# Pairing the heads of two batches by the engine of their scores, and opening layer two's memory nine steps earlier

## The chip, the cores and the metric

The kernel runs on one core of a Trainium2 chip. The metric is the device time of one execution in microseconds; the time before is 929.59 us, the median of three runs (927.67 to 930.28). TensorE is called PE in the rows, VectorE DVE, ScalarE ACT, GpSimd POOL, SyncE SP.

## The reference, cut to what matters

An attention of 4 batches, 8 heads, 576 positions and 64 values per head is followed by two feed-forward layers on 2304 tokens (512 to 2048 to 512). The attention is the sum of two: one over q, k and v pooled by four positions (144 by 144), and one over a band of seven keys around each position.

```python
def sm_attn(qq, kk, vv):
    s = scale * np.matmul(qq, kk.transpose(0, 1, 3, 2))
    s = s - np.max(s, axis=-1, keepdims=True)
    a = np.exp(s)
    a = a / (np.sum(a, axis=-1, keepdims=True) + 1e-09)
    return np.matmul(a, vv)
q_d = q.reshape(B, H, Sd, factor, D).mean(axis=3)
out_up = np.repeat(sm_attn(q_d, k_d, v_d), factor, axis=2)
mask = np.abs(pos[:, None] - pos[None, :]) < factor
scores = np.where(mask, scale * np.matmul(q, k.transpose(0, 1, 3, 2)), -1000000000.0)
...
attn_out = (out_up + out_local).astype(np.float32)
x = attn_out.transpose(0, 2, 1, 3).reshape(B * S, H * D)
h = x @ w_in;  x = (np.maximum(h, 0.0) + alpha * np.minimum(h, 0.0)) @ w_out
h = x @ w_in2; g = np.where(h > 0.0, h, np.exp(np.minimum(h, 0.0)) - 1.0)
out = g @ w_out2
```

`k_d` and `v_d` are made as `q_d`; `out_local` is softmax(scores) times v.

## The kernel before, in words

**Stages.** Layer 1 is the backbone: 2304 tokens in eight groups of 288, two per batch, and for each group 16 tiles of the 2048 hidden values. One tile is a *step*; there are 128, numbered from 0, and from step 32 on each group is 16 steps (groups of batch three at 64 and 80, of batch four at 96 and 112). A step has twelve input matmuls (`mm_in`, L415; 128x288, operands split into a high and a low part, `xh`, `xl`, `wi`), an activation on ACT and DVE (`th_elem`, L1422: `n`, `r`, `gh`, `gl`) and, two steps later, twelve output matmuls (`out1`, L1450; `gh`, `gl`, `wo`). Layer 2 works in 40 *units* u of four per turn of 512 tokens (`upf` L1706, `down2` L1743): seven products of half size in place of eight, on `xq` and `wi`, then the output with `wo`.

**Attention** of a batch runs between the matmuls of the group before. Its heads are taken in four pairs p of two. Per pair the q and k (`qk`) and v (`vv`) are loaded, pooled by DVE, and the pooled attention is computed (`th_pair` L1066, `th_da` L1103): scores `sm`, softmax `P`, its transposes `pt`, v transposed `vs`, and the weighted sum (`dav_mm` L761, two heads on the two halves of the output's rows), copied to `od` by ACT (`dav_ev` L770). The banded scores of a pair are eight blocks of 72 queries by 78 keys (`s_mm` L569): a matmul with 64 rows of contraction per block and head, four blocks to a bank, copied by ACT to `ss` (`s_ev` L578), written to DRAM `scr` (`s_write` L585) and read back as a band `sd`. In batches three and four (b = 2 and 3 in the code) only head 1 of each pair goes that way; head 0 is scored by DVE (`SDVE` L91, `th_SD` L1041, `s_dve` L533), from its own loads `kls` and `qls`. In batch two both heads go to PE. Band softmax and weighted sum of batches three and four are DVE's (`acc`, `pr`, `vl`); PE transposes `acc` (`x_tp` L797) and DVE adds `od` into `x`, which the next group reads. While layer 1 runs, attention has two PSUM banks.

**Order.** No engine's order is written by hand. `fused_kernel` keeps threads with a priority each, and a clock of its own (`_Clock`, L94) with a cost for every operation: PE work of a thread is put between layer 1's matmuls when the clock has its operands ready (`pe`, L918), ACT and DVE work when those engines come to it (`advance`, L876). For a matmul of a head in the upper half of the array's rows the clock counts 8 ns (L265), since it takes its partner to run beside it; for a load it counts a byte per 1/360 ns (L232). All loads go through SP's one queue, in program order.

**Memory.** Attention's tiles are in a pool `pA`. At step T7 = 112 (L821, L1880) it is closed, layer 2's pool `pC` takes its place, and layer 2's threads start: `th_ldw2` (L1364) loads raw weights into slots that layer 1 sets free one by one from step 112 on, `decode` (L1309) makes them 32 bits wide (`cp` on ACT, `cp` and `cw` on DVE), `th_conv_in` (L1331) forms four differences `S` and four split tiles `wi`, `th_conv_out` (L1355) two `wo` per set of weights, and `th_x2` (L1502) prepares the tokens `x`, `xt`, `xq`.

Of the kernel before, what the change touches and what calls it, by code (L numbers as in the profile page):

```python
# [7 lines left out]
F32 = mybir.dt.float32  # L8
# [3 lines left out]
U64 = mybir.dt.uint64  # L12
# [6 lines left out]
S = 576  # L19
D = 64  # L20
# [23 lines left out]
DP = -14.7  # L44
NP0 = -14.6
STEP = 1.0
G2 = 512
U2 = G2 // 2
XR = 11
# [39 lines left out]
PN = 1, 5  # L89
NB = 2  # L90
SDVE = {2: (0,), 3: (0,)}  # L91


class _Clock:  # L94
# [208 lines left out]
def fused_kernel(ctx: ExitStack, tc: tile.TileContext, qk, vt, vl, ql, kl, vb, w_in1, w_out1, alpha,  # L303
# [281 lines left out]
    def s_write(b, p, k0, n, t, rs):  # L585
        for i, r in enumerate(rs):
            u0 = p * (NU // 2) + k0
            SP.dma_start(out=scr[b, r][u0:u0 + n, 0:BLK * KW].rearrange("u (q k) -> q u k", k=KW), in_=t[:, i, 0:n])

    def band(t):  # L590
# [179 lines left out]
    def dav_ev(key, bk):  # L770
        b, p, qs = key
        if ("od", b) not in st:
            st["od", b] = Ap.tile([128, NP, SD], F32, tag="od", name="od", bufs=2)
        ACT.activation(out=st["od", b][:, p, qs[0] * 72:(qs[-1] + 1) * 72], in_=bk[:, 0:len(qs) * 72], func=AF.Copy)

    def av_ops(b, u, i):
        t0 = u * HT + i * TS
# [81 lines left out]
    def finish(*key):  # L859
        done[key] = ck.cur["t"]  # L860
# [157 lines left out]
                SP.dma_start(out=xsp, in_=st["x", 0, 0].rearrange("p k t j -> p k (t j)"))  # L1018

    def th_S(b, p):  # L1020
        rs = tuple(r for r in range(2) if r not in SDVE.get(b, ()))
        yield "key", "ld", b, p
        for i in range(2):
            yield "tok", "ss"
            bks = yield "bank", len(rs)
            s_mm(b, p, 4 * i, 4, bks, rs)
            if i == 1:
                finish("smm", b, p)
            yield ("ACT",)
            t = s_ev(4, bks)  # L1030
            release(bks)
            yield ("SP",)
            if b < NB:
                s_write0(b, p, i, t)
                finish("S", b, p, i)
            else:
                s_write(b, p, 4 * i, 4, t, rs)
            put("ss")
        finish("S", b, p)
# [19 lines left out]

    def th_qk(b, p):  # L1060
        yield "key", "sq", b, p
        if len(SDVE.get(b, ())) < 2:
            yield "key", "smm", b, p
        put("qk")

# [37 lines left out]
    def th_da(b, p, qs):  # L1103
        key = (b, p, qs)
        yield "tok", "P"
        bks = yield "bank", 2
        sd_mm(b, p, qs, bks)
        if b:
            put("sm")
        yield ("ACT",)  # L1110
        sd_ev(key, bks)
        release(bks)
        yield ("DVE",)
        sd_max(key)
        yield ("ACT",)
        sd_exp(key)
        yield ("DVE",)
        sd_rec(key)
        yield ("DVE",) if b < DN else ("ACT",)
        sd_norm(key, b < DN)  # L1120
        yield "tok", "pt"
        bks = yield "bank", 2
        pt_mm(key, bks)
        put("P")
        yield ("ACT",)
        pt_ev(key, bks)
        release(bks)
        yield "key", "vs", b, p
        bks = yield "bank", 1
        dav_mm(key, bks[0])  # L1130
        put("pt")
        if b:
            put("vs")
        else:
            finish("dav", p, qs)
        yield ("ACT",)
        dav_ev(key, bks[0])
        release(bks)
        finish("od1", b, p, qs)
        if all(("od1", b, z, qs) in done for z in range(NP)):  # L1140
            finish("od", b, qs[-1])

    def th_da0(p):
        yield "key", "sq", 0, p
# [22 lines left out]
    def th_soft(b):  # L1167
        yield "key", "sal", b
        for r in range(2):
            if r in SDVE[b]:  # L1170
                for u in range(2):
                    for i in range(HT // TS):
                        yield "key", "SD", b, u, i, r
            else:
                for p in range(NP):
                    yield "key", "S", b, p
        yield ("SP",)
        s_read(b)
# [183 lines left out]
        finish("wo", q, z)  # L1362

    def th_ldw2():  # L1364
        for q in range(NQ):
            for nm, z in (("i", 0), ("i", 1), ("o", 0), ("o", 1)):
                slot = wslot[q % NJ][z + (4 if nm == "o" else 0)]
                yield "key", "fr", q // NJ, slot
                yield ("DMA",)
                key = (2, nm, q % NP2 * 2 + z, q)  # L1370
                load_w(key, slot)
                finish("ld", key)
                ck.cur["t"] = now[0]

# [432 lines left out]
    with tc.manual_schedule():  # L1807
# [37 lines left out]
            spawn(th_conv(k), k / CS, early=ECONV)  # L1845
        for b in range(1, B):
            g0 = 32 * (b - 1)
            for p in range(NP):
                if len(SDVE.get(b, ())) < 2:
                    spawn(th_S(b, p), g0 + OS + p if b > 1 else P1 + p / 4)  # L1850
                spawn(th_qk(b, p), -20)
                spawn(th_pair(b, p), g0 + OP + p if b > 1 else P1 + p / 4, g0 + 2 * p + OPS if b > 1 else ST1 + ST2 * p)
            if b < NB:
                for u in range(2):
                    q = PN[u] + 32 * (b - 1)
# [18 lines left out]
        for s in range(NS1):  # L1874
            slot[0] = s if s else -1
            ly, g, f, first, last, i = seq[s]
            if s == 1:
                avail[:] = bank[6:8]
                banks[:] = [x for x in banks if any(x[0] is z for z in avail)]
            if s == T7:  # L1880
                assert all(t["p"] < -50 for t in threads), [t["w"] for t in threads]
                pA.__exit__(None, None, None)
                pC = tc.tile_pool(name="pC", bufs=1)
# [86 lines left out]
def _prepare(np, a):  # L1970
# [4 lines left out]
    for i, x in enumerate((q, k)):  # L1975
        qk[:, :, :, i, HALO:HALO + S] = x.transpose(0, 1, 3, 2).reshape(B, NP, 128, S)
    vt = v.transpose(0, 1, 3, 2).reshape(B, NP, 128, S)
    vp = np.zeros((B, H, SPAD, D), f4)
    vp[:, :, HALO:HALO + S] = v
    vl = np.stack([vp[:, :, NT * j:NT * j + NT + 2 * HALO] for j in range(CH)], axis=2)  # L1980
# [67 lines left out]
```

## Time and profile before

| what | value |
|---|---|
| median of three runs (lowest, highest) | 929.59 us (927.67, 930.28) |
| the profiled execution, its span | 928.21 us, 926.4 us |
| TensorE matmuls in flight; weight loads | 903.6 us (98%); 831.4 us (90%) |
| DVE, ACT, POOL busy | 721.1 us (78%), 523.3 us (56%), 2.9 us |
| moved by DMA | 106.36 MB, 115 GB/s mean |
| granted clock of TensorE, mean | 0.99 |

The span runs from the first to the last instruction; 1.8 us of the execution lie around it. Matmuls are pipelined, so a busy TensorE is not one at its peak, and the cost of a matmul in a stream is the distance between starts. An idle engine that nobody waits for costs nothing; a wait of TensorE does, in this kernel.

### The profile page before, as it was taken

Reading aid. Unit: us, or ns where it says so; the run is one execution under the profiler, and the core shown is the slowest. Engines: PE = TensorE matmul, PEld = TensorE weight load, DVE = VectorE, ACT = ScalarE, POOL = GpSimd, SP = SyncE. Lnnn points to the kernel's source line nnn. Section 1 sums busy time; section 2 is a strip of 40 time slices with the busy share of each in tenths; the row PEclk is TensorE's granted clock in tenths of the full one; section 3 lists DMA queues with packets and bytes.
Section 4 is the critical chain, followed back from the end, with each engine's and each line's share of the span. In section 5 each row is a group of like instructions: output and inputs, shape, how many; then the busy total and the mean of one; then the engine's idle time right before and its main releaser. Section 6 shows DMA issues by size and latency. Waiting matters only on the chain.

```text
span 926.4 us, 17510 instructions
## 1 busy us (share of the span) xinstructions
PE 903.6 (98%) x6721; PEld 831.4 (90%) x6721; DVE 721.1 (78%) x1552; ACT 523.3 (56%) x1312; POOL 2.9 (0%) x6
## 2 busy tenths in 40 slices
PE   8798999999999999999999998999999999999998
PEld 5577989999998999999999997899998988899987
DVE  6788986438778899899537999979797559989753
ACT  6798786645335642323236667656675456756543
POOL 0000000000000000000100000000000000000000
PEclk8899999999999999999999999999999999999999
DMA  9757816443122413010113751414324144242502
GB/s 267 274 213 270 273 31 97 125 132 100 46 71 66 145 49 107 27 37 32 47 36 106 227 186 54 155 46 137 98 85 125 36 157 140 84 160 80 182 12 79
DMA packets 69417, 106.36 MB, mean 115 GB/s; under 512 B 26610, under 2 KB 43378, under 8 KB 69154
## 3 DMA queue, kind: packets, MB, share of 16 engines
q1 hardware_dynamic: 69334, 105.25, 36.8%
q8 instruction: 52, 0.85, 0.4%
q14 instruction: 31, 0.25, 0.1%
HBM read 86.89 MB, written 19.78 MB: 115 GB/s over the span
## 4 chain that ended last, share of the span: by engine, by line
PE 80%; DVE 6%; ACT 6%; DMA 5%; issue 2%; SPq 0%; DVEq 0%; ACTq 0%
PE bank L298 80%; DMA qk<-in_qk_dram 2%; DMA rawi<-in_w_in_dram 1%; ACT dP L298 1%; DVE cw L298 1%; ACT wo L298 1%; DVE cp L298 1%; DVE wi L298 1%; DMA out_dram<-os 1%; ACT cp L298 1%; ACT n L298 1%; ACT cw L298 1%; ACT wi L298 1%; DVE gl L298 1%; ACT P L298 1%
## 5 line engine op out<-in xcount | busy, mean ns | idle before, releaser
L298 PE MATMUL bank<-xh,wi 128*128 128x288 f32 x976 | 223.8, 300 | 0.6 <-DVE wi L298 0.6
L298 PE MATMUL bank<-gh,wo 128*128 128x288 f32 x976 | 222.2, 299 | 1.3 <-ACT ys L298 1.3
L298 PEld LDWEIGHTS bank<-xq,wi 128*128 128x128 f32 x1536 | 195.7, 192 | 10.8 <-ACT wi L298 2.0
L298 PE MATMUL bank<-xq,wi 128*128 128x256 f32 x1536 | 198.7, 284 | 3.5 <-ACT wi L298 1.6
L298 ACT ACTIVATE n<-bank 128x288 f32<-128x288 f32 (+1 forms) x176 | 70.6, 401 | 200.0 <-PE bank L298 197.8
L298 PE MATMUL bank<-wo,gh 128*128 128x512 f32 x576 | 179.3, 392 | 0.1
L298 PEld LDWEIGHTS bank<-gh,wo 128*128 128x128 f32 x976 | 165.0, 188 | 5.0 <-ACT ys L298 2.1
L298 PEld LDWEIGHTS bank<-xh,wi 128*128 128x128 f32 x976 | 164.8, 188 | 4.8 <-issue 2.7
L298 PE MATMUL bank<-gl,wo 128*128 128x288 f32 x488 | 144.6, 296 | 0.3 <-DVE gl L298 0.2
L298 PE MATMUL bank<-xl,wi 128*128 128x288 f32 x488 | 143.7, 294 | 0.0
L298 PEld LDWEIGHTS bank<-wo,gh 128*128 128x128 f32 x576 | 103.3, 189 | 17.8 <-ACT gh L298 0.3
L298 PE MATMUL bank<-wo,gl 128*128 128x512 f32 x288 | 112.3, 390 | 0.2 <-DVE gl L298 0.2
L298 DVE SCALAR_TENSOR_TENSOR r<-n,nal,bank 128x288 f32<-128x288 f32 x128 | 65.2, 510 | 57.9 <-ACT n L298 57.2
L298 PEld LDWEIGHTS bank<-gl,wo 128*128 128x128 f32 x488 | 92.0, 188 | 0.8 <-DVE gl L298 0.8
L298 PEld LDWEIGHTS bank<-xl,wi 128*128 128x128 f32 x488 | 92.0, 188 | 0.2
L298 ACT ACTIVATE gh<-r 128x288 fp32r<-128x288 f32 x122 | 54.1, 443 | 65.3 <-DVE r L298 65.2
L298 DVE TENSOR_TENSOR gl<-r,gh 128x288 fp32r<-128x288 f32 x122 | 55.4, 454 | 17.4 <-ACT gh L298 16.9
L298 PEld LDWEIGHTS bank<-wo,gl 128*128 128x128 f32 x288 | 54.1, 188 | 12.5 <-DVE gl L298 0.8
L298 DVE TENSOR_TENSOR gl<-n,gh 128x512 fp32r<-128x512 f32 (+1 forms) x80 | 50.6, 634 | 9.4 <-ACT gh L298 8.5
L298 DVE TENSOR_TENSOR c<-m,bank 128x256 f32<-128x256 f32 x64 | 26.4, 419 | 36.0 <-PE bank L298 35.7
L298 ACT ACTIVATE gh<-n 128x512 fp32r<-128x512 f32 (+1 forms) x80 | 46.3, 582 | 12.4 <-DVE n L298 12.0
L298 ACT ACTIVATE n<-n 128x512 f32<-128x512 f32 (+1 forms) x80 | 47.2, 590 | 2.5
(125 smaller groups left out, 1215.0 us busy)
## 6 DMA issues: line engine op xcount, KB each, us to landing
rawi<-in_w_in_dram SPq DMA_DIRECT2D x40, 512.0 KB
rawo<-in_w_out_dram SPq DMA_DIRECT2D x40, 512.0 KB
qk<-in_qk_dram SPq DMA_DIRECT2D x12, 582.0 KB
x<-yT SPq DMA_DIRECT2D x8, 576.0 KB
osp<-os SPq DMA_DIRECT2D x18, 256.0 KB
os<-osp SPq DMA_DIRECT2D x18, 256.0 KB
out_dram<-os SPq DMA_DIRECT2D x18, 256.0 KB
yT<-ys SPq DMA_DIRECT2D x28, 144.0 KB
```

Source lines behind the costliest of these rows:

```text
L298: return fn(*args, **kw)
```

## The change

**Heads.** For batches three and four the host puts the eight heads in the order 0, 2, 4, 6, 1, 3, 5, 7. Pairs 0 and 1 then hold the four heads that DVE scores, pairs 2 and 3 the four that PE scores, and a score block has both heads of a pair (`th_S` only for pairs 2 and 3; `th_qk` lets the load of pairs 0 and 1 go behind the pooling). Pairs are taken in the order 0, 2, 1, 3. Since pairs 0 and 2 share two output tiles of heads in their first order, the weighted sum of the pooled attention waits for both (`th_dav`) and is one block of eight matmuls with one copy.

**Memory.** `pA` is closed at step TC = 103 in place of 112; an assertion there says that no thread of attention is left. Layer 2's first six raw tiles go to the buffers `n`, `gh`, `gl` of `pC` (`raws`), which layer 2 needs later, and wait for no weight slot.

```diff
--- before.py
+++ after.py
@@ -44,6 +44,8 @@
 DP = -14.7
 NP0 = -14.6
 STEP = 1.0
+TC = 103
+STG = ("n", "gh", "gl", "n", "gh", "gl")
 G2 = 512
 U2 = G2 // 2
 XR = 11
@@ -89,6 +91,8 @@
 PN = 1, 5
 NB = 2
 SDVE = {2: (0,), 3: (0,)}
+QUAD = {2, 3}
+QORD = 0, 2, 1, 3
 
 
 class _Clock:
@@ -585,6 +589,8 @@
     def s_write(b, p, k0, n, t, rs):
         for i, r in enumerate(rs):
             u0 = p * (NU // 2) + k0
+            if b in QUAD:
+                u0, r = (2 * p + r - NP) * (NU // 2) + k0, 1
             SP.dma_start(out=scr[b, r][u0:u0 + n, 0:BLK * KW].rearrange("u (q k) -> q u k", k=KW), in_=t[:, i, 0:n])
 
     def band(t):
@@ -772,6 +778,21 @@
         if ("od", b) not in st:
             st["od", b] = Ap.tile([128, NP, SD], F32, tag="od", name="od", bufs=2)
         ACT.activation(out=st["od", b][:, p, qs[0] * 72:(qs[-1] + 1) * 72], in_=bk[:, 0:len(qs) * 72], func=AF.Copy)
+
+    def dav2_mm(b, i, bk):
+        t = {(r, e): st.pop(("pt", r, b, i + e * (NP // 2), (0, 1))) for r in range(2) for e in range(2)}
+        for r in range(2):
+            for kh in range(2):
+                for e in range(2):
+                    PE.matmul(out=bk[e * D:(e + 1) * D, r * SD:(r + 1) * SD],
+                              lhsT=st["vs", b, i + e * (NP // 2)][:, kh, r * D:(r + 1) * D], rhs=t[r, e][:, kh, :],
+                              start=(kh == 0), stop=(kh == 1))
+
+    def dav2_ev(b, i, bk):
+        if ("od", b) not in st:
+            st["od", b] = Ap.tile([128, NP, SD], F32, tag="od", name="od", bufs=2)
+        ACT.activation(out=st["od", b][:, 2 * i:2 * i + 2], in_=bk[:, 0:2 * SD].rearrange("q (a k) -> q a k", a=2),
+                       func=AF.Copy)
 
     def av_ops(b, u, i):
         t0 = u * HT + i * TS
@@ -1018,7 +1039,7 @@
                 SP.dma_start(out=xsp, in_=st["x", 0, 0].rearrange("p k t j -> p k (t j)"))
 
     def th_S(b, p):
-        rs = tuple(r for r in range(2) if r not in SDVE.get(b, ()))
+        rs = (0, 1)
         yield "key", "ld", b, p
         for i in range(2):
             yield "tok", "ss"
@@ -1059,7 +1080,7 @@
 
     def th_qk(b, p):
         yield "key", "sq", b, p
-        if len(SDVE.get(b, ())) < 2:
+        if b not in QUAD or p >= NP // 2:
             yield "key", "smm", b, p
         put("qk")
 
@@ -1125,6 +1146,9 @@
         yield ("ACT",)
         pt_ev(key, bks)
         release(bks)
+        if b in QUAD:
+            finish("pt", b, p)
+            return
         yield "key", "vs", b, p
         bks = yield "bank", 1
         dav_mm(key, bks[0])
@@ -1140,6 +1164,23 @@
         if all(("od1", b, z, qs) in done for z in range(NP)):
             finish("od", b, qs[-1])
 
+    def th_dav(b, i):
+        for p in (i, i + NP // 2):
+            yield "key", "pt", b, p
+            yield "key", "vs", b, p
+        bks = yield "bank", 1
+        dav2_mm(b, i, bks[0])
+        for z in range(2):
+            put("pt")
+            put("vs")
+        yield ("ACT",)
+        dav2_ev(b, i, bks[0])
+        release(bks)
+        for p in (i, i + NP // 2):
+            finish("od1", b, p, (0, 1))
+        if all(("od1", b, z, (0, 1)) in done for z in range(NP)):
+            finish("od", b, 1)
+
     def th_da0(p):
         yield "key", "sq", 0, p
         yield from th_da(0, p, (0, 1))
@@ -1172,7 +1213,7 @@
                     for i in range(HT // TS):
                         yield "key", "SD", b, u, i, r
             else:
-                for p in range(NP):
+                for p in range(NP // 2 if b in QUAD else 0, NP):
                     yield "key", "S", b, p
         yield ("SP",)
         s_read(b)
@@ -1362,13 +1403,20 @@
         finish("wo", q, z)
 
     def th_ldw2():
+        k = 0
         for q in range(NQ):
             for nm, z in (("i", 0), ("i", 1), ("o", 0), ("o", 1)):
                 slot = wslot[q % NJ][z + (4 if nm == "o" else 0)]
-                yield "key", "fr", q // NJ, slot
+                key = (2, nm, q % NP2 * 2 + z, q)
+                if k >= len(STG):
+                    yield "key", "fr", q // NJ, slot
                 yield ("DMA",)
-                key = (2, nm, q % NP2 * 2 + z, q)
-                load_w(key, slot)
+                if k < len(STG):
+                    raw[key] = cp["pool"].tile([128, 512], U64, tag=STG[k], name="raws", bufs=2)
+                    SP.dma_start(out=raw[key], in_=wsrc[2, nm][key[2]])
+                else:
+                    load_w(key, slot)
+                k += 1
                 finish("ld", key)
                 ck.cur["t"] = now[0]
 
@@ -1845,11 +1893,15 @@
             spawn(th_conv(k), k / CS, early=ECONV)
         for b in range(1, B):
             g0 = 32 * (b - 1)
-            for p in range(NP):
-                if len(SDVE.get(b, ())) < 2:
-                    spawn(th_S(b, p), g0 + OS + p if b > 1 else P1 + p / 4)
+            for z in range(NP):
+                p = QORD[z] if b in QUAD else z
+                if b not in QUAD or p >= NP // 2:
+                    spawn(th_S(b, p), g0 + OS + z if b > 1 else P1 + z / 4)
                 spawn(th_qk(b, p), -20)
-                spawn(th_pair(b, p), g0 + OP + p if b > 1 else P1 + p / 4, g0 + 2 * p + OPS if b > 1 else ST1 + ST2 * p)
+                spawn(th_pair(b, p), g0 + OP + z if b > 1 else P1 + z / 4, g0 + 2 * z + OPS if b > 1 else ST1 + ST2 * z)
+            if b in QUAD:
+                for i in range(NP // 2):
+                    spawn(th_dav(b, i), g0 + OP + 2 * i + 1)
             if b < NB:
                 for u in range(2):
                     q = PN[u] + 32 * (b - 1)
@@ -1877,7 +1929,7 @@
             if s == 1:
                 avail[:] = bank[6:8]
                 banks[:] = [x for x in banks if any(x[0] is z for z in avail)]
-            if s == T7:
+            if s == TC:
                 assert all(t["p"] < -50 for t in threads), [t["w"] for t in threads]
                 pA.__exit__(None, None, None)
                 pC = tc.tile_pool(name="pC", bufs=1)
@@ -1975,6 +2027,11 @@
     for i, x in enumerate((q, k)):
         qk[:, :, :, i, HALO:HALO + S] = x.transpose(0, 1, 3, 2).reshape(B, NP, 128, S)
     vt = v.transpose(0, 1, 3, 2).reshape(B, NP, 128, S)
+    for b in QUAD:
+        hs = [0, 2, 4, 6, 1, 3, 5, 7]
+        vt[b] = v[b, hs].transpose(0, 2, 1).reshape(NP, 128, S)
+        for i, x in enumerate((q, k)):
+            qk[b, :, :, i, HALO:HALO + S] = x[b, hs].transpose(0, 2, 1).reshape(NP, 128, S)
     vp = np.zeros((B, H, SPAD, D), f4)
     vp[:, :, HALO:HALO + S] = v
     vl = np.stack([vp[:, :, NT * j:NT * j + NT + 2 * HALO] for j in range(CH)], axis=2)
```

PE, the first scores of batch three (`bank<-qk`), in steps 33 and 34. Before, two blocks of one head:

```order
L298 MATMUL bank_71<-xh,wi_651 128x288
L298 MATMUL bank_73<-qk 72x78 x4
L298 MATMUL bank_71<-xh,wi_651 128x288
L298 MATMUL bank_71<-xl,wi_651 128x288
L298 MATMUL bank_71<-xh,wi_651 128x288
L298 MATMUL bank_72<-qk 72x78 x4
L298 MATMUL bank_71<-xh,wi_651 128x288
L298 MATMUL bank_71<-xl,wi_651 128x288
L298 MATMUL bank_71<-xh,wi_651 128x288
```

Now:

```order
L302 MATMUL bank_70<-xh,wi_734 128x288
L302 MATMUL bank_72<-qk 72x78
L302 MATMUL bank_73<-qk 72x78
L302 MATMUL bank_72<-qk 72x78
L302 MATMUL bank_73<-qk 72x78
L302 MATMUL bank_72<-qk 72x78
L302 MATMUL bank_73<-qk 72x78
L302 MATMUL bank_72<-qk 72x78
L302 MATMUL bank_73<-qk 72x78
L302 MATMUL bank_70<-xh,wi_734 128x288
```

The rows alternate between two banks, one per head; the other three blocks of a batch read alike.

ACT, steps 102 to 104 of layer 1 (`n` opens a step). Before:

```order
L298 ACTIVATE n<-bank_70 128x288
L298 ACTIVATE gh<-r 128x288
L298 ACTIVATE n<-bank_71 128x288
L298 ACTIVATE gh<-r 128x288
L298 ACTIVATE n<-bank_70 128x288
L298 ACTIVATE gh<-r 128x288
```

Now:

```order
L302 ACTIVATE n<-bank_70 128x288
L302 ACTIVATE gh<-r 128x288
L302 ACTIVATE cp<-raws 128x512 x2
L302 ACTIVATE n<-bank_71 128x288
L302 ACTIVATE cp<-raws 128x512 x2
L302 ACTIVATE gh<-r 128x288
L302 ACTIVATE cp<-raws 128x512
L302 ACTIVATE n<-bank_70 128x288
L302 ACTIVATE cp<-raws 128x512
L302 ACTIVATE gh<-r 128x288
```

Six copies `cp` of staged tiles stand between the `gh` of layer 1; on SP their loads `raws` follow the result writes of batch three and stand ahead of the loads of `x`.

DVE, layer 2, between the `m` of u=2 and the `m` of u=3 (`wi` is the low part of a weight tile that u=3 reads). Before, the last 12 of 32 rows:

```order
L298 TENSOR_TENSOR wi_7228<-cw,wi_7228 128x512
L298 SCALAR_TENSOR_TENSOR n<-n,c 128x512
L298 TENSOR_TENSOR gl<-n,gh 128x512 x2
L298 TENSOR_TENSOR wi_7246<-S,wi_7246 128x512
L298 TENSOR_SCALAR cp<-cp 128x512
L298 SCALAR_TENSOR_TENSOR cw<-rawi_7021,cp 128x512
L298 TENSOR_SCALAR cp<-cp 128x512
L298 TENSOR_TENSOR wi_7256<-S,wi_7256 128x512
L298 SCALAR_TENSOR_TENSOR cw<-rawo_7069,cp 128x512
L298 TENSOR_TENSOR wi_7263<-cw,wi_7263 128x512
L298 TENSOR_SCALAR cp<-cp 128x512
L298 SCALAR_TENSOR_TENSOR cw<-rawi_7044,cp 128x512
```

Now, the first 12 of 23:

```order
L302 TENSOR_TENSOR m<-s_7138,bank_70 128x256
L302 TENSOR_TENSOR xq_7114<-xt,xq_7114 128x512
L302 TENSOR_TENSOR e<-m,bank_71 128x256
L302 TENSOR_TENSOR c<-e,bank_72 128x256
L302 TENSOR_TENSOR wi_7146<-cw,wi_7146 128x512
L302 TENSOR_TENSOR xt<-x_6845 128x512
L302 TENSOR_TENSOR gl<-n,gh 128x512
L302 TENSOR_SCALAR cp<-cp 128x512
L302 TENSOR_TENSOR wi_7183<-S,wi_7183 128x512
L302 SCALAR_TENSOR_TENSOR cw<-rawo_6988,cp 128x512
L302 TENSOR_TENSOR xq_7186<-xt,xq_7186 128x512
L302 TENSOR_TENSOR c<-m,bank_71 128x256
```

The first two `wi` move from the 21st and 24th row to the 5th and 9th; the `cp`, `cw` and `S` of later tiles leave this stretch.

## Rows read from the trace of the kernel before

**Rows 1.** The page: busy time by engine; the chain that ended last, by engine.

```profile
PE 903.6 (98%) x6721; PEld 831.4 (90%) x6721; DVE 721.1 (78%) x1552; ACT 523.3 (56%) x1312; POOL 2.9 (0%) x6
...
PE 80%; DVE 6%; ACT 6%; DMA 5%; issue 2%; SPq 0%; DVEq 0%; ACTq 0%
```

**Rows 2.** Waits of PE, 180 to 480 us: total us, times, longest.

```profile
PE bank L298 <- DMA qk<-in_qk_dram: 0.3, 1, 0.3
PE bank L298 <- ACT P L298: 0.2, 1, 0.2
```

**Rows 3.** Timeline of PE: start us, us, instruction, xcount; batch three's scores.

```profile
253.46 0.29 PE L298 MATMUL bank<-gh,wo 128*128 128x288 f32 x1
253.68 0.77 PE L298 MATMUL bank<-qk 64*72 64x78 f32 x8
...
254.62 0.29 PE L298 MATMUL bank<-gl,wo 128*128 128x288 f32 x1
254.75 0.29 PE L298 MATMUL bank<-gh,wo 128*128 128x288 f32 x1
```

**Rows 4.** Timeline of PE: batch two's scores, both heads of a pair.

```profile
136.10 0.29 PE L298 MATMUL bank<-xh,wi 128*128 128x288 f32 x1
136.32 0.77 PE L298 MATMUL bank<-qk 64*72 64x78 f32 x16
...
137.40 0.29 PE L298 MATMUL bank<-xh,wi 128*128 128x288 f32 x1
```

**Rows 5.** All score matmuls of PE, 190 to 322 us (ns min/median/max).

```profile
L298 PE MATMUL bank<-qk x128: 225/228/285, 195.0 to 318.3; 64*72 64x78 f32 x128
```

**Rows 6.** Timeline of PE: weighted sums of the pooled attention, one pair.

```profile
232.80 0.30 PE L298 MATMUL bank<-gh,wo 128*128 128x288 f32 x1
233.03 0.72 PE L298 MATMUL bank<-pt,vs 72*64 72x144 f32 x8
...
234.05 0.29 PE L298 MATMUL bank<-gh,wo 128*128 128x288 f32 x1
```

**Rows 7.** PE at layer 2; windows: length, busy PE, PEld, DVE, ACT, POOL; PEclk.

```profile
550.35 3.04 PE L298 MATMUL bank<-xq,wi 128*128 128x256 f32 x24
...
562.64 0.50 PE L298 MATMUL bank<-xq,wi 128*128 128x256 f32 x2 [1.61 <-ACT wi L298]
564.49 4.29 PE L298 MATMUL bank<-xq,wi 128*128 128x256 f32 x22 [1.35 <-DVE wi L298]
...
532.38:535.25 2.87, 2.87 (x26) 2.87 (x25) 2.84 (x8) 1.88 (x4) 0.00 (x0) 1.00 0.98 325
562.64:568.58 5.94, 4.59 (x25) 4.39 (x26) 5.77 (x11) 4.03 (x9) 0.00 (x0) 0.74 0.00 0
```

**Rows 8.** Windows of the hole before layer 2, its start, and attention.

```profile
450.00:480.00 30.00, 30.00 (x228) 30.00 (x227) 10.29 (x23) 9.35 (x23) 2.69 (x2) 1.00 0.14 36
500.00:560.00 60.00, 59.42 (x423) 56.59 (x422) 56.85 (x120) 42.02 (x89) 0.00 (x0) 1.00 0.53 168
...
180.00:450.00 270.00, 269.43 (x2169) 259.09 (x2168) 222.20 (x493) 114.85 (x334) 0.00 (x0) 1.00 0.25 72
```

**Rows 9.** Window from DVE's `m` of u=2 to that of u=3.

```profile
552.47:568.67 16.20, 13.24 (x75) 11.71 (x74) 15.99 (x35) 10.90 (x22) 0.00 (x0) 0.90 0.05 18
```

**Rows 10.** Timelines of SP and ACT: two weight tiles loaded back to back.

```profile
490.36 1.91 SPq L298 DMA_DIRECT2D rawo<-in_w_out_dram  x2
...
494.91 0.67 ACT L298 ACTIVATE cp<-rawo 128x512 f32<-128x512 f32 x1
498.15 0.68 ACT L298 ACTIVATE cp<-rawo 128x512 f32<-128x512 f32 x1 [2.58 <-DMA rawo<-in_w_out_dram]
```

**Rows 11.** Copies of score banks by ACT, 190 to 322 us (ns min/median/max).

```profile
L298 ACT ACTIVATE ss<-bank x16: 410/427/431, 195.8 to 320.4; 72x312 f32<-72x312 f32 x16
```

**Rows 12.** Timeline of PE: a transposition block of batch four.

```profile
414.98 0.49 PE L298 MATMUL bank<-ident,acc 128*128 128x128 f32 x3
```

## The prediction

> **What bounds the kernel.** I read the engine summary and the chain that ended last first [rows 1]: TensorE has matmuls in flight for 903.6 of 926.4 us, and 80% of the chain is TensorE's own stream, with no more than 6% by any other engine. So a matmul that is taken out shortens the run unless something that TensorE doesn't wait for now becomes late. The list of TensorE's waits tells how near that is: from 180 to 480 us, the stretch of attention for batches two to four, it waits 0.5 us in all [rows 2]. Then I read TensorE's timeline where the edits fall: the score blocks of batch three, the same blocks of batch two, where both heads of a pair already go to TensorE, and the start of layer 2. Batches are counted from one here; the code's b is one less.
>
> **Scores, removed.** In batches three and four a block of four score matmuls for one head (8 records, each matmul is two) stands in the stream of layer 1. The reader should take the distance between starts of the main matmuls around it, since ends are modelled [rows 3]: from 253.46 to 254.75 us is 1.29 us for three main steps that take 0.13 us each, so the block costs 1.29 - 0.40 = 0.89 us. In batch two a block holds twice the records, two heads on the two halves of the array's rows, and costs 137.40 - 136.10 - 0.40 = 0.90 us [rows 4]. Twice the work in the same time. There are 128 such records [rows 5], so 16 blocks of 8; the change makes 8 of 16. Saved: 16 x 0.89 - 8 x 0.90 = **7.0 us**. Copies out of the banks, writes and DVE's own scores keep their number; DVE's heads are the same heads as before, only renamed in the halves.
>
> **Weighted sums of the pooled attention, merged.** Per pair, 8 records cost 234.05 - 232.80 - 0.40 = 0.85 us [rows 6]; batches three and four have 8 such blocks, 6.8 us. Afterwards 4 blocks hold 16 records each. Within a block a further pair of matmuls adds (0.72 - 0.29) / 3 = 0.14 us (the block's length less one matmul's, over the three pairs behind the first), so a block of 16 costs 0.85 + 4 x 0.14 = 1.41 us and four cost 5.6: saved **1.2 us**. Bounds: 16 records that don't overlap in pairs would add 12 x 0.14 to 0.85, which is 2.5 us a block, a loss of 3.3 us in all; a block that cost no more than one of 8 would gain 3.4. I take the paired value, since the new order alternates the two halves of the output's rows and the old one overlapped without that. The copies of `od` fall from 8 to 4, on an idle part of ACT, at nothing.
>
> **Waits of the score blocks.** Two of the sixteen waited, 0.3 and 0.2 us [rows 2]. With half the blocks and the loads of the first two pairs let go before any score, I take 0.3 us saved, between 0 and 0.5.
>
> **The handover to layer 2.** At u=3, the fourth unit of the new layer, TensorE stood 1.61 us for ACT's high part of a `wi` tile and 1.35 us for DVE's low part, and then ran 22 matmuls slowly [rows 7]: the granted clock of that stretch is 0.74, between the levels of 1.2 and 2.4 GHz, where the same 24 matmuls of u=0, at a granted clock of 1.00, took 2.87 us. Here they took 4.59 without the waits, so 1.72 us went to the clock behind them. Together 1.61 + 1.35 + 1.72 = 4.7 us. The cause is DVE: busy 56.85 of 60 us from 500 to 560, yet only 10.29 of 30 from 450 to 480, ACT 9.35 [rows 8]. The change starts layer 2's decoding in that hole, on six staged tiles. What it is worth is read from the order of DVE: between the `m` of u=2 and that of u=3 there stand 33 instructions now and 23 then, three `cp`, four `S`, three `cw` and one `wo` fewer and one `gl` more; the two `wi` writes that u=3 needs first stand 21st and 25th now, behind nearly everything, and 5th and 9th then. The stretch from the one `m` to the other is 16.2 us now, 0.49 per instruction [rows 9], so the 9th is done some 4.4 us behind `m`, where TensorE reaches u=3 about 8.6 us behind it (its stream ends at 562.64 - 1.61 = 561.03). So 4 us of cover stand where 3 us were missing, and I take the whole **4.7 us**. Bounds: 0, if DVE comes to `m` later by those 4 us, and 5.3 with the small DVE waits nearby. DVE is late next, if at all, at u=4; I charge **0.5 us** for new small waits there (0 to 4.7, rival two).
>
> **What is added and moved.** Six loads of 512 KB go onto SP's queue before the three loads of `x` and before the four result writes of the last segment but one; they wait for the last reader of attention's memory (step 100), and what is queued behind them is needed some 12 steps later at the earliest. On ACT six copies `cp` now stand between the `gh` of steps 102 to 104. The chip's price for tiles loaded back to back: issue at 490.36, first copy at 494.91, the second held by the DMA until 498.15, with a `gh` behind it, and TensorE not held by it [rows 10]. So 4.6 us for the first and at most 3.2 for each further one. If all six are spaced so, the sixth arrives 4.6 + 5 x 3.2 = 20.6 us behind the issue, which is about when TensorE needs the `gh` of step 104 (six steps of 24 matmuls at 0.13 us, 19 us). I take no cost: even with every tile at the pessimistic spacing the last one misses by 1.6 us. The other end is rival three. The Trainium skill (DMA: Bandwidth & Descriptors, Specifications) gives a limit of about 358 GB/s of memory traffic for a core; by it six tiles would take an estimated 8.8 us, no copy would be late, and this term would be 0 at both ends. The row, 0.52 MB in 3.2 us, is less than half of that rate. Two subtractions that POOL did go to DVE, 1.4 us in its idle stretch: nothing.
>
> **Sum.** 7.0 + 1.2 + 0.3 + 4.7 - 0.5 = 12.7 us. The profiled execution took 928.2 us (926.4 and 1.8 around it), so 915.5. The median of the runs shown, 929.6, is 1.4 us above the profiled one and they spread by 2.6; I add nothing for that and forecast **915.5 us**.
>
> **Rival one: the banks are emptied too slowly.** A paired block takes both banks that attention has in layer 1, and ACT empties them one behind the other, 0.43 us each [rows 11]. If TensorE's next small block waits for the second each time, 8 x 0.43 = 3.4 us are lost: 918.9. The Trainium skill (TensorEngine Tiling (Array Packing), PSUM Bottleneck) warns of this: tiling speeds up the matmuls and not the evacuation, which may become the bottleneck. The trace speaks against it: the blocks of batch two have the same two banks, and cost 0.90 us [rows 4]. Chance 0.08.
>
> **Rival two: the wait at u=3 moves on.** Behind the `m` of u=4 DVE's order now has 25 instructions (21 before), 12 us at 0.49, against TensorE's 10.7 for a unit (550.35 to 561.03 [rows 7]). If DVE falls behind there, the wait and the slow clock come back and 4.7 is not gained: 915.5 + 4.7 - 0.5 = 919.7. Against it: the unit before has 19 and the one behind 21, so the excess is spread, and 4 us of cover stand ahead of it. Chance 0.12.
>
> **Rival three: ACT stands behind the staged loads** and the `gh` of step 104 or 105 is late: 1.6 us, with a slow clock behind it of the size seen at u=3, 1.7: 918.8. It needs every tile to take 3.2 us. Chance 0.07.
>
> **Rival four, slower: DVE can't keep the earlier order.** The changed order puts the third transposition block of batch four's first half at step 88, four steps before its place now (414.98 us, step 92 [rows 12]). TensorE works in order: if DVE has that `acc` no earlier than now, TensorE stands there for four steps of 24 x 0.13 us, 12.5 us, plus the 8 us by which it comes earlier: 928.2 - 12.7 + 20.5 = 936. It decides against the change once DVE is more than 12.7 us behind TensorE at one of these blocks. Against it: DVE is busy 222 of 270 us there [rows 8], the scores that batch three's softmax waits for end four steps earlier (step 44, not 48), and DVE's own list moves up with them; 39 us of idle time remain after the cut. Chance 0.07, of which 0.04 loses the whole gain and 0.03 most of it.
>
> That the change doesn't do what it says, heads not overlapping, is excluded by batch two's blocks.
>
> **How the numbers follow.** Forecast 0.66, rivals 0.08, 0.12, 0.07 and 0.07. A measurement of this kernel tells 0.3%, 2.8 us, from no change. The forecast and the first three rivals all lie below 921 and are faster: 0.93; of rival four 0.03 ends within 0.3% and 0.04 slower. The range goes from the better bounds of all terms (7.0 + 3.4 + 0.5 + 5.3 = 16.2, 912.0, and 0.5 for the spread of the runs) up to the rivals (919.7, and 1.3 for the spread): 911.5 to 921.0.
>
> **What would show it.** Score records of batches three and four in 8 blocks of 16 of 0.9 us; four blocks of 16 `pt,vs` of about 1.4; no TensorE wait above 0.3 us and no fall of the granted clock at u=3; DVE busier by some 7 us in the hole before layer 2 (4 `cp`, 4 `cw`, 4 `S`, 2 `xt`); first matmul of layer 2 about 8 us earlier, of u=4 about 13. I am wrong if TensorE waits over 2 us in total for DVE between steps 33 and 103, or if the block costs 1.3 or more.

## The result, and the profile after

The change takes 917.13 us (median of 4 runs, 915.86 to 917.44) and the kernel before, on the same chip, 929.13 us: a ratio of 0.987, 95% interval 0.985 to 0.989, 12.0 us less. The forecast was 915.5, in a range of 911.5 to 921.0. The profiled execution has a span of 915.5 us, where before had 926.4.

The engine summary of the page after, the chain that ended last [rows 1], and the same chain on the page of a second execution of the change (`e11_change` below):

```profile
PE 896.8 (98%) x6721; PEld 827.4 (90%) x6721; DVE 722.6 (79%) x1554; ACT 522.1 (57%) x1308; POOL 0.2 (0%) x4
...
PE 73%; DVE 2%; DMA 1%; ACT 0%; issue 0%; SPq 0%; ACTq 0%; DVEq 0%
...
PE 89%; ACT 4%; DMA 3%; DVE 2%; issue 1%; SPq 0%; ACTq 0%; DVEq 0%
```

TensorE still bounds, and has the same 6721 matmul records: nothing was taken out of its list, only the time of blocks and waits. The first chain is followed back only to 207.8 us, 77% of the span, so its 73% are not to be set beside the 80% of before; the second goes back to the start, and there TensorE has 89%. TensorE's timeline at a score block of batch three and at a merged block of weighted sums (start us, length, instruction, count), to be set beside [rows 3, 4, 6]:

```profile
232.76 0.29 PE L302 MATMUL bank<-gh,wo 128*128 128x288 f32 x1
232.99 0.77 PE L302 MATMUL bank<-qk 64*72 64x78 f32 x16
...
234.06 0.42 PE L302 MATMUL bank<-gh,wo 128*128 128x288 f32 x2
...
201.43 0.29 PE L302 MATMUL bank<-xh,wi 128*128 128x288 f32 x1
201.65 1.20 PE L302 MATMUL bank<-pt,vs 72*64 72x144 f32 x16
...
203.14 0.29 PE L302 MATMUL bank<-xh,wi 128*128 128x288 f32 x1
```

By the prediction's own measure, start to start less three main steps, the paired block costs 234.06 - 232.76 - 0.40 = 0.90 us and the merged one 203.14 - 201.43 - 0.40 = 1.31. All blocks of a kind, added up: scores of batches three and four 14.5 us before (16 blocks) and 8.5 now (8 blocks); weighted sums 6.7 before and 5.3 now. TensorE's waits from 180 to 475 us [rows 2] show what is in those 8.5:

```profile
PE bank L302 <- ACT ys L302: 0.8, 1, 0.8
PE bank L302 <- ACT P L302: 0.7, 1, 0.7
```

The second is one score block (207.83 us) that stood until ACT had emptied a bank of `P`; with what surrounds the gap it cost 1.06 us. Without it the eight blocks would stand at 7.4. The first, 0.77 us at 325.48, costs 0.9 with its surroundings and is new: the five traces with this order of TensorE that are read below have it, and none with unpaired heads has.

The start of layer 2 in TensorE's timeline, and windows (length; busy PE, PEld, DVE, ACT, POOL; then the granted clock, the DMA share and GB/s), beside [rows 7, 8]:

```profile
554.20 3.04 PE L302 MATMUL bank<-xq,wi 128*128 128x256 f32 x24
...
578.99 0.73 PE L302 MATMUL bank<-wo,gh 128*128 128x512 f32 x2 [0.74 <-ACT gh L302]
579.89 0.50 PE L302 MATMUL bank<-wo,gl 128*128 128x512 f32 x1 [0.16 <-DVE gl L302]
...
442.00:472.00 30.00, 30.00 (x228) 30.00 (x228) 15.34 (x33) 10.96 (x24) 0.00 (x0) 1.00 0.32 113
490.00:550.00 60.00, 60.00 (x436) 58.17 (x435) 50.46 (x105) 39.38 (x80) 0.00 (x0) 1.00 0.47 151
554.20:560.00 5.80, 5.80 (x39) 5.31 (x38) 5.70 (x12) 4.02 (x8) 0.00 (x0) 1.00 0.00 0
```

At u=3 no wait stands in the row of 24 any more and the granted clock behind it is 1.00. DVE does 15.3 us in the hole where it did 10.3, and is busy 50.5 of 60 us around layer 2's start where it was busy 56.9. A smaller wait has come up 25 us later.

To see where the time came from, the run is cut at three places that exist in every kernel of this study: step 22 of layer 1 (its first matmul; the stretch before it differs by some us from one execution to the next), the first matmul of layer 2, and the last matmul. Times in us, from the starts in each trace:

| profiled execution of | step 22 to layer 2 | layer 2 to the end |
|---|---|---|
| before | 390.6 | 389.9 |
| the change | 384.4 | 385.2 |
| the change, a second execution | 382.8 | 384.8 |

Attention gave 6.2 us (7.8 in the second execution), the handover 4.7 to 5.1.

### The profile page after: what moved, and what is told of

It reads as the page before. It is cut to its first block, busy times and chain, and to the rows that moved or that the text cites. A ratio compares the mean times of both kernels' runs of the same rounds, so it can differ in the third digit from the quotient of the medians.

```text
span 915.5 us, 17475 instructions
## 1 busy us (share of the span) xinstructions
PE 896.8 (98%) x6721; PEld 827.4 (90%) x6721; DVE 722.6 (79%) x1554; ACT 522.1 (57%) x1308; POOL 0.2 (0%) x4
## 4 chain that ended last, share of the span: by engine, by line
PE 73%; DVE 2%; DMA 1%; ACT 0%; issue 0%; SPq 0%; ACTq 0%; DVEq 0%
PE bank L302 73%; DMA out_dram<-os 1%; DMA rawi<-in_w_in_dram 1%; DVE cw L302 0%; DVE n L302 0%; DVE os L302 0%; DVE gl L302 0%; DVE S L302 0%; ACT P L302 0%; DVE cp L302 0%; DVE x L302 0%; DVE wi L302 0%; DVE wo L302 0%; ACT gh L302 0%; DVE c L302 0%
## 5 line engine op out<-in xcount | busy, mean ns | idle before, releaser
L302 PE MATMUL bank<-xq,wi 128*128 128x256 f32 x1536 | 196.7, 283 | 0.3 <-DVE c L302 0.3
L302 DVE TENSOR_TENSOR gl<-r,gh 128x288 fp32r<-128x288 f32 x122 | 55.3, 453 | 12.4 <-ACT gh L302 11.4
```

Of the source, the lines that this page charges most:

```text
L302: return fn(*args, **kw)
```

## The experiments

### The paired heads alone

`e1_heads` and `e7_heads_again` are one kernel:

```diff
-TC = 103
-STG = ("n", "gh", "gl", "n", "gh", "gl")
+TC = 112
+STG = ()
```

> The paired heads of batches three and four alone; layer 2's memory is opened at step 112 again, without staged tiles. My theory: the two parts add up. In the trace of the change the blocks between main matmuls cost 6.0 us less in all, so this kernel takes 929.1 - 6.1 = 923.0 us, TensorE reaches u=3 6 us earlier than before, and the wait there with its slow clock (1.6 + 1.35 us and about 1.7) is back. Rival: DVE is what layer 2's start waits for, it was busy 56.85 of 60 us there, so that a TensorE that comes 6 us earlier only waits 6 us longer at u=3: 928 to 929 us.

> The paired heads alone a second time, for its trace (the first trace is of a disturbed execution). 922 us as measured; TensorE at u=3 as before, two waits of 1.3 to 1.6 us and a granted clock of about 0.74 behind them, 4 to 5 us together, against none in the change. Rival: the wait is smaller there than before, since the paired heads end the attention four steps earlier and leave DVE more room, 2 us or less, and the rest of the difference to the change lies elsewhere.

Measured: 921.74 and 921.23 us, ratios 0.993 (0.991 to 0.995) and 0.992 (0.990 to 0.995) to before: 6.6 to 7.1 us less. TensorE at u=3 in the second run's trace, and the window behind it:

```profile
557.81 0.51 PE L302 MATMUL bank<-xq,wi 128*128 128x256 f32 x2 [1.60 <-ACT wi L302]
559.66 4.64 PE L302 MATMUL bank<-xq,wi 128*128 128x256 f32 x20 [1.35 <-DVE wi L302]
...
557.81:563.70 5.89, 4.54 (x21) 4.34 (x22) 5.72 (x11) 3.98 (x9) 0.00 (x0) 0.60 0.00 0
```

The two waits are those of before to 0.01 us [rows 7], at a time 5 us earlier: DVE's work for layer 2 starts behind step 112 and moved up with TensorE. Both rivals fall. Step 22 to layer 2 takes 383.4 us, layer 2 389.9, as before.

### The memory alone

```diff
-QUAD = {2, 3}
+QUAD = set()
...
-        rs = (0, 1)
+        rs = tuple(r for r in range(2) if r not in SDVE.get(b, ()))
```

> The early memory with six staged tiles alone; the heads stay unpaired, and TensorE's order is word for word that of before. My theory: no wait at u=3 and a granted clock of 1.00 behind it, so 1.61 + 1.35 + 1.72 = 4.7 us less, 924.4 us (924 to 925.5 with a small new wait two units later). Rival: the wait only moves on to u=4 or u=5, as a wait of 0.7 us in the trace of the change hints, and 929 us stay.

Measured: 930.03 us, ratio 1.002 (1.001 to 1.004): **slower**, by 2 us, and my theory of a plain sum falls, though not as the rival has it. Layer 2 takes 384.6 us, so all of the handover's gain is there; but step 22 to layer 2 takes 396.5, 5.9 more than before. The trace shows one wait, in SP's, ACT's and TensorE's timelines and two windows:

```profile
449.59 0.81 SPq L302 DMA_DIRECT2D raws<-in_w_in_dram  x2
...
453.30 0.67 ACT L302 ACTIVATE cp<-raws 128x512 f32<-128x512 f32 x1 [2.88 <-DMA raws<-in_w_in_dram]
458.55 0.66 ACT L302 ACTIVATE cp<-raws 128x512 f32<-128x512 f32 x1 [4.58 <-DMA raws<-in_w_in_dram]
...
460.87 0.61 PE L302 MATMUL bank<-xh,wi 128*128 128x288 f32 x1 [4.04 <-DVE r L302]
...
450.50:460.50 10.00, 6.34 (x48) 6.08 (x47) 2.75 (x6) 2.26 (x5) 0.00 (x0) 0.93 1.02 360
460.87:466.00 5.13, 5.13 (x22) 5.13 (x23) 5.06 (x12) 3.00 (x7) 0.00 (x0) 0.52 0.32 96
```

ACT's second copy does not read the second tile: it waits for the semaphore of the fifth load, the first tile of the second set of weights. That load landed at 458.53 us, 8.9 us behind the first issue, where the second had landed at 454.49. Layer 1's `n` stood behind the copy on ACT; DVE's `r` needs that `n`, and TensorE a bank that `r` empties. TensorE stood 4.04 us and then ran at a granted clock of 0.52, the lower of its two levels, for the next 5.1 us. The same rows of the change:

```profile
435.95 1.01 DVE L302 TENSOR_TENSOR x<-bank,od 128x64 f32<-128x64 f32 x3 [0.27 <-PE bank L302]
...
437.03 2.23 SPq L302 DMA_DIRECT2D raws<-in_w_in_dram  x2
...
444.89 0.65 ACT L302 ACTIVATE cp<-raws 128x512 f32<-128x512 f32 x1
448.22 0.66 ACT L302 ACTIVATE cp<-raws 128x512 f32<-128x512 f32 x1 [2.68 <-DMA raws<-in_w_in_dram]
```

There the loads go out 7.9 us ahead of step 103, at whose start the copies stand (its first matmul starts at 444.91 us), and with the memory alone 0.7 us ahead of it (450.33): the paired heads let DVE's last use of attention's memory stand two steps further up, at 435.95 us, where it starts at 448.48 before. Of these 12.5 us, 5.4 are TensorE's own lead at step 103, the rest is order. ACT stood 2.68 us for the fifth tile here too (it landed at 448.20), but TensorE did not wait. To load that tile second was not tried; by the marks with the memory alone it would have been there some 4 us sooner (an estimate from 454.49 and 458.53).

### The memory alone, with later copies

On top of the edit above, the planner's landing time for a staged tile is put off:

```diff
+LATE = 8000.0
...
+                if k < len(STG):
+                    ck.cur["t"] += LATE
                 k += 1
                 finish("ld", key)
```

> The memory part alone again, with one number changed: the planner takes the staged tiles to land 8 us later, so that five of ACT's six copies stand two to four steps further down its order; TensorE's and SP's orders and the issue of the loads are as in the run with the memory alone. My theory of why that run gained nothing: the loads waited for the last read of attention's memory, 449.6 us, and landed 3.7 to 9 us later, but ACT's copies stood right behind, so that ACT stood 4.6 us, TensorE 4.0 us with a slow clock behind it, 6.5 us in all, which ate the gain at u=3. Then this kernel loses that wait and keeps the gain: 930 - 6.5 = 923.5 us, between 923 and 925. Rival: the loads themselves are in the way (their traffic, or the queue of SP with the loads of x behind them), and 930 us stay.

Measured: 931.94 us, 1.004 (1.003 to 1.006). The rival is right: with ACT's copies out of the way the next load in SP's queue holds the same place. DVE's and TensorE's timelines:

```profile
465.25 0.69 DVE L303 TENSOR_TENSOR xt<-x 128x512 f32<-128x512 f32 x1 [6.56 <-DMA x<-yT]
...
467.15 0.61 PE L303 MATMUL bank<-xh,wi 128*128 128x288 f32 x1 [5.09 <-DVE r L303]
```

`x` comes in three loads, the first issued 3.1 us behind the first staged tile; the last of them landed 13.5 us behind that tile's issue, and `xt`, which reads `x`, stands ahead of `r` on DVE.

### The memory alone, with later copies and later reads of x

The edit above with 11000, and the same for the load of `x`; the orders of TensorE and of SP stay those of the memory alone.

```diff
+        if not i:
+            ck.cur["t"] += LATE
         if not z:
             for kt in range(KT):
```

> The memory part alone, with the planner told that both the staged tiles and the load of x behind them land 11 us later than it thinks: ACT's copies 2 to 6 stand three to four steps further down, and DVE's two subtractions that read x stand about four steps further down. TensorE's order and SP's order are as in the run with the memory alone, and the loads go out at the same point. My theory: all that ate the gain of the memory part alone was work on ACT and DVE that stood ahead of layer 1's own work and waited for loads that are let go only at step 102 and share the DMA engines for 12 us. Then no TensorE wait is left between steps 103 and 112, u=3 has none either, and the time is 928.4 - 4.7 = 923.7 us (922.5 to 925). Rival: something else of the early opening costs 5 to 6 us (the traffic itself, or a further wait behind these two), and the time stays at 930 us or above.

Measured: 924.69 us, 0.996 (0.994 to 0.997), 4.1 us less than before. TensorE's waits from 440 to 600 us are those that the change has, and no more:

```profile
PE bank L303 <- ACT gh L303: 0.7, 1, 0.7
PE bank L303 <- DVE gl L303: 0.2, 1, 0.2
```

That settles the memory part: it is worth 4.7 to 5.3 us in layer 2, and takes them back in layer 1 where work on loads let go too late stands ahead of layer 1's own on ACT and DVE. In the table below this kernel still takes 1.2 us more than before from step 22 to layer 2, but that lies ahead of the edits, where it waited 1.4 us for a load of `qk`; from step 103 to layer 2 it takes 81.3 us, with 82.1 before and 87.8 with the memory alone.

| profiled execution of | step 22 to layer 2 | layer 2 to the end |
|---|---|---|
| heads alone | 383.4 | 389.9 |
| memory alone | 396.5 | 384.6 |
| memory, later copies | 398.4 | 385.0 |
| memory, later copies and reads of x | 391.8 | 384.6 |
| change without staged tiles | 384.6 | 388.7 |

### The change without staged tiles

```diff
-STG = ("n", "gh", "gl", "n", "gh", "gl")
+STG = ()
```

> The change with layer 2's memory opened at step 103, but no staged tiles: the first loads wait for slots that come free from step 112 on, as before. My theory: it is the staged tiles that let DVE and ACT work in the hole, so the wait at u=3 is back and the time is that of the paired heads alone, 923 us. Rival: the earlier opening is what counts (more buffers for the decoding from the start), and 917 us stay.

Measured: 918.97 us, 0.991 (0.989 to 0.992), between the two theories. Layer 2 takes 388.7 us: of the 4.7 that the memory part gives there, the earlier opening brings 1.2 and the staged tiles 3.5. By the ratios alone it is 1.8 and 3.4 us, and the first of these is no wider than the intervals. TensorE's waits of 500 to 620 us are smaller pieces than those of u=3:

```profile
PE bank L302 <- DVE gl L302: 1.8, 2, 0.9
PE bank L302 <- ACT gh L302: 0.9, 1, 0.9
PE bank L302 <- DVE wi L302: 0.6, 1, 0.6
```

### One half behind the other

```diff
-        for k in range(k0, k0 + n):
-            for bk, r in zip(bks, rs):
+        for bk, r in zip(bks, rs):
+            for k in range(k0, k0 + n):
...
-        for r in range(2):
-            for kh in range(2):
-                for e in range(2):
+        for e in range(2):
+            for r in range(2):
+                for kh in range(2):
```

> The change with another order within a block: the scores of all four tiles of one head and then those of the other, where the change has the two heads in turn; and the merged weighted sums with one half of the output's rows first and then the other. My theory: two matmuls share the array only where neighbours in the stream lie on different halves of it. Then each of the 16 score blocks goes from 0.90 us to about 1.7 (twice the 0.89 of one head, less what a block loses once), 16 x 0.8 = 13 us, and the four merged blocks from 1.32 to between 1.6 and 2.5 us, 1 to 5 us: 931 to 935 us. Rival: what halves the cost is something else, such as the number of blocks or of banks, and the time stays at 917 us.

Measured: 923.59 us, 0.995 (0.993 to 0.997), 7.4 us slower than the change by the ratios; half of what my theory said. A block of scores and a merged block in its trace:

```profile
131.69 1.10 PE L302 MATMUL bank<-qk 64*72 64x78 f32 x16
...
226.78 1.74 PE L302 MATMUL bank<-pt,vs 72*64 72x144 f32 x16
```

The score block costs 1.22 us and not 1.7, the merged one 1.87: 16 x 0.32 + 4 x 0.55 = 7.3 us, the whole difference. The two halves overlap best where they stand side by side in the stream; in this order the second head's first record starts when three of the first head's eight are still to come. And the stream is not all of a block: of the 0.77 us of eight records [rows 3] the first start to the last start is 0.77 - 0.23 = 0.54 (228 ns is one record [rows 5]); the other 0.89 - 0.54 = 0.35 is paid once per block for the way in and out. The Trainium skill (TensorEngine Tiling (Array Packing), Tiling Modes) says that changing the tiling mode drains TensorE; it gives no number. That the 0.35 us go with the form of the array and not with any small block is borne out by the transposes, which use more than half of it in rows and columns. One of them in the change's trace:

```profile
154.24 0.29 PE L302 MATMUL bank<-gh,wo 128*128 128x288 f32 x1
154.37 0.67 PE L302 MATMUL bank<-ident,P 72*72 72x72 f32 x8
...
155.18 0.43 PE L302 MATMUL bank<-gh,wo 128*128 128x288 f32 x2
```

Eight records cost 155.18 - 154.24 - 0.40 = 0.54 us, no more than their stream; in the same way three `ident,acc` cost 0.33 and six 0.66, nothing per block, while a block of 16 `ppT,vb` (78*64) costs 0.85 and one of 32 1.35, which leaves 0.35 for the block. So pairing saves about 0.54 us of stream and 0.35 of the way in and out.

### Three attempts at a better version

`e6_change_later` is the change with the first `LATE` edit above (8000), `e8_ready` has the edit below, `e10_best` has both; `e11_change` is the change itself beside them.

```diff
-PM = 300.0
+PM = 700.0
```

> The change with the same number changed (staged tiles taken to land 8 us later). In the change ACT stood 2.7 us for the second tile and TensorE did not wait, because the loads went out 9 us before their copies. My theory: nothing to gain there, and the copies are still early enough for u=3: the time of the change, within 1 us. Rival: decoding that begins two steps later is late at u=3 again: 2 to 4 us slower than the change.

> The change, with the planner's rule tightened: a small block goes to TensorE only when its inputs are 0.7 us old, not 0.3. My theory: the change lost 1.06 us at a score block that waited for ACT's copy of P, 0.47 at a block that waited for a load of pp and 0.2 at another score block, because the planner places blocks too close behind their inputs; with this rule these go, and one block is merged with a neighbour: 1.5 to 2 us less than the change. Rival: each block is placed later, later work is late in its turn, and nothing or a loss comes out.

> The change with both of the small edits that did no harm: staged tiles taken to land 8 us later, and small blocks sent only when their inputs are 0.7 us old. My theory: each takes away a chance of a wait and neither adds a block; 914.5 to 916 us, up to 2 us below the change. Rival: the waits they avoid are as often not there in the change, and the two are the same within 1 us.

> The change itself, unaltered, beside the two other runs on the same chip, as their measure: 916 to 917 us, 0.987 of the kernel before. Any theory gives the same here; how far this run and the first measurement of the change lie apart tells how small a difference the two runs beside it can show.

Measured: 916.21 us, 0.988 (0.986 to 0.989); 915.62, 0.987 (0.985 to 0.989); 916.82, 0.987 (0.985 to 0.989); and the change 917.24, 0.987 (0.985 to 0.989). None differs from the change. With the tighter rule TensorE waits 1.8 us for `ys`, 1.1 for `pp` and 0.4 for `P` from 100 to 475 us: the waits changed places. And the wait for `P` at the second score block is not in every execution: of five traces with that order of TensorE (the change twice, `e3_nostage`, `e6_change_later`, `e7_heads_again`) two have it, the change's first and that of `e3_nostage`. It begins with a load. DVE's product of `kls` and `qls` (the scores that DVE makes) waits for that load, in the change's first trace and in its second:

```profile
205.30 0.63 DVE L302 TENSOR_TENSOR spr<-kls,qls 128x448 f32<-128x448 f32 x1 [4.52 <-DMA qls<-in_ql_dram]
...
203.62 0.62 DVE L302 TENSOR_TENSOR spr<-kls,qls 128x448 f32<-128x448 f32 x1 [2.73 <-DMA qls<-in_ql_dram]
```

Behind it stand DVE's `r`, ACT's `gh` and then the copy of `P`; where `qls` was there at 203.62, the block started at 207.16 without a wait.

## Why the prediction was right, and where not

- **Scores, 7.0 us and 0.3 of waits.** Right: 14.5 us became 8.5 in the first trace and 7.2 to 7.4 in three others without the wait for `P`. "Twice the work in the same time" holds to 0.01 us.
- **Weighted sums, 1.2 us.** Measured 1.4 (6.7 to 5.3). A block of 16 is 1.32 us, not 1.41: a further pair adds 0.12 us, not 0.14; the upper bound, 2.5, was not reached even in the order with one half behind the other (1.87).
- **Not in the sum.** The new order splits two blocks of 32 `ppT,vb` records, 1.35 us each, into two of 16, 0.84 and 0.85 us: 0.7 us, two more ways in and out. And the new wait for `ys`, 0.9 us with its surroundings.
- **The handover, 4.7 us less 0.5.** Right. Against the usual 5.62, 5.94 or 8.37 us, the distances between every 24th input matmul show that the waits and the clock cost 0.5, 4.3 and 0.7 us before, 5.5 together, and nothing now; the new wait, 0.74 and 0.16 us, costs 1.4 with what surrounds it. It is rival two's mechanism, but 25 us behind u=3 and without a fall of the clock. Layer 2 as a whole is 4.7 us shorter; the rest of it, 0.7 us, are two waits for DVE near 775 us before.
- **The staged loads, no cost.** Right in number, wrong in its reason. I took the tiles to land 4.6 us behind the issue and then 3.2 each [rows 10], with the last of them as the one that could be late. The 3.2 was no spacing of two loads: the second of [rows 10] was issued 1.6 us behind the first. The staged tiles land in the order of their issue, 1.3 to 1.45 us apart from the second on, and the sixth was there 10.3 us behind the issue with the memory alone and 12.6 in the change, not 20.6. The one that holds ACT is the fifth, since the second copy reads it: after 8.9 us and 11.2. What decides is how far ahead of ACT's copies and of the reads of `x` the loads are let go, and that lead is not the memory part's own: the paired heads give it. I added the two parts as if each stood by itself, so that nothing was lost in the change is in part luck. Alone, they gave 6.6 to 7.1 us and a loss of 2; together 12.
- **Rival three** has the right place and the wrong condition: slow tiles are not needed, only loads that go out at step 102 in place of step 100. Its price would have been 6 us and not 3.
- **Rivals one and four** did not come: no block behind a paired one waited for its second bank, and no transposition block waited for DVE. The wait for `P` is a wait for a bank, too, but of the paired block itself, and a late load was behind it. TensorE's waits for DVE in steps 33 to 103 are below the threshold of the list.
- **The signs.** Layer 2's first matmul came 6.2 us earlier (7.2 in the second execution) and not 8, u=4's 11.6 (12.4) and not 13, and DVE did 5.0 us more in the hole and not 7.
- **The sum.** Up to layer 2 7.2 + 1.4 - 0.7 - 0.9 + 0.6 = 7.6 us, with the scores of the traces without the wait for `P`; the 0.6 are two waits for `gl`, at 506.49 and 530.81 us before, that are gone. In layer 2 5.5 - 1.4 + 0.7 = 4.8. Together 12.4, where the medians differ by 12.0 and the forecast had 12.7; the table has 12.9 for the second execution and 10.9 for the first, with its wait for `P`. The 915.5 was counted from the profiled execution; from the median of before, 929.13, the same 12.7 give 916.4.

## What to carry to other kernels

Two edits that look independent can hang together: with the planner's order as it was, the tiles staged early paid only because the other edit ended the use of their memory two steps sooner; alone they paid once the work on them was put off. So price a load by the instructions that stand ahead of other work in their engines' order and wait for it, see which load each of them reads (here the second copy read the fifth tile), and look at every load behind it in the queue, not only at the last tile. Where matmuls on half the array are strewn between full ones, count the blocks as well as the records: here 0.35 us of 0.89 belonged to the block.

## What the runs showed of the hardware

- Six tiles of 512 KB, issued from SP's queue within 3 us, landed one behind the other in the order of their issue: with the memory alone 3.6, 4.9, 6.2, 7.6, 8.9 and 10.3 us behind the first issue (a load's semaphore rises in sixteen steps, and the last counts). From the second to the sixth that is 2.1 MB in 5.41 us, 388 GB/s; the window of 10 us above has 360 in the mean, with the loads of `x` in it. The Trainium skill (DMA: Bandwidth & Descriptors, Specifications) gives a limit of about 358 GB/s of memory traffic for a core. The window's mean is at it, the tiles by themselves came faster, and my reading of 0.52 MB in 3.2 us as the chip's price for one tile was wrong.
- In these stretches the granted clock fell with the wait ahead of it: 1.00 in the 42 us that hold the wait of 0.74 us (558 to 600 us of the change), 0.60 to 0.74 over 6 us behind waits of 1.6 and 1.35 us, 0.52 over 5.1 us behind one of 4.04 us.
